# Output products with the weight as the stationary operand, and the result turned back on the way out

## The chip, the cores and the metric

The kernel runs on one core of one Trainium2 chip. The metric is device time in microseconds (us), the median of three runs. A core has a matrix engine (TensorE, here PE, with its weight loads shown apart as PEld), a vector engine (DVE), a scalar engine (ACT), GpSimd (POOL) and an engine that only issues transfers (SP). A matrix product loads a stationary operand of 128 columns, then streams a moving operand past it; the result goes to PSUM, from which DVE or ACT must copy it before a transfer can store it.

## The reference

Per batch (4) and head (8), a complex state of 48 x 48 is decayed, updated with k and v and read with q over 768 steps. The heads' outputs, side by side, are the rows x (3072 x 384) of a gated feed-forward layer:

```
S_re, S_im = decay(S_re, S_im, a_t) + k_t v_t^T      y_t = q_t S_re
g = x @ w_gate ; silu = g / (1 + exp(-g))
out = (silu * (x @ w_val)) @ w_out                    # w_out: 1536 x 384, float32 result
```

## The kernel before

The steps are cut into 24 slabs of 128 positions, two slabs to a group, so 12 groups of 256 positions. For each group, stage_ops computes decays and rotations on DVE and ACT, slab_ops makes scores, state products and outputs on PE (line 691 and its neighbours) and leaves x for 256 positions, split into a high part xh and a low part xl that the fast matrix format can hold. Weights are split in the same way.

ffn_ops(g) then runs 12 steps f for each group, one for each 128 of the 1536 hidden columns:

- f1 (line 942): 18 products, each with 128 columns of w_gate or w_val as the stationary operand and the 256 positions of xh or xl as the moving one (128x256), into the PSUM tile gv;
- silu on ACT (line 948), the gating product on DVE (line 953), then the split of the gated tile into hh (cast) and hl (difference);
- f2 (line 976): for each half of the group, three products with 128 positions of hh or hl as the stationary operand and the 384 columns of w_out as the moving one (128x384), so six to a step. They add up over the 12 steps in two PSUM tiles p_po, one for each half.

After step 11, oe copies each half out of PSUM (ACT line 354 or DVE line 356), and os stores its 128 rows with one transfer from SP (line 990). Group 0 works with unsplit operands (two products of line 976 to a step), and groups 1 to 11 with split ones.

A planner (plan, lines 120 to 206) simulates all engines with a table of costs and due times and writes one fixed order for each engine. Every engine then takes its instructions in that order and waits in place where an operand is missing. On PE the order is f1 of step f+1, then f2 of step f, so that silu, gating and split of a step run beside other products; scores, state products and cumulations stand in between. Step 0 of a group's f2 writes the PSUM tiles that oe of the group before must have read.

Some tiles are padded so that operands lie at chosen places: xh, xl, hh and hl have 128 columns more than they need and start 16 columns in (GATED, INPUT), and the f1 weights are allotted from a pool that a dummy tile of 96 columns (STILL) shifts. All other sizes are multiples of 128 columns. So the start of a moving operand lies, modulo 128 columns, 16 - 96 = 48 columns behind that of its stationary operand in f1, and 0 - 16 = 112 behind it in f2.

Of the kernel before, what the change touches and what calls it, by code (L numbers as in the profile page):

```python
# [9 lines left out]
F32 = mybir.dt.float32  # L10
# [44 lines left out]
WIDE_KEYS = 64  # L55
TURNS = P // WIDE_KEYS

TURN_OVER, STILL, GATED, INPUT = 128, 96, 16, 16
HIGH, LOW, WHOLE = 0, 1, 2
SHY = -5.6765  # L60
POOL_FROM = 9.8274
# [169 lines left out]
def quick(ctx, tc, q, k, v, a_re, a_im, w_gate, w_val, w_out, out, count):  # L231

    nc = tc.nc
    PS = bass.MemoryType.PSUM
    const = ctx.enter_context(tc.tile_pool(name="const", bufs=1))
    still = ctx.enter_context(tc.tile_pool(name="still", bufs=1))
    gap = ctx.enter_context(tc.tile_pool(name="gap", bufs=1))
    work = ctx.enter_context(tc.tile_pool(name="work", bufs=1))
    dram = ctx.enter_context(tc.tile_pool(name="dram", bufs=4, space=bass.MemoryType.DRAM))
    psum = ctx.enter_context(tc.tile_pool(name="psum", bufs=1, space=PS))  # L240
# [16 lines left out]
    G = const.tile([96, B, H, 64], F32, name="G")  # L257
    vts = [const.tile([P, H, 64], F32, name=f"vt{i}") for i in range(2)]
    turned_v = [const.tile([P, 2, 2, 64], F32, name=f"vr{i}") for i in range(2)]
    still.tile([P, STILL], F32, name="ahead")  # L260
    gap.tile([P, TURN_OVER - STILL], F32, name="behind")
    W, HALVES = {}, {}
    WIDE = {"w": 2 * DM, "o": DM}

    def place(nm, f, dtype):

        pool = still if nm == "w" else work
        return pool.tile([P, 2 * WIDE[nm]], dtype, name=f"w{nm}{f}", tag=f"w{nm}{f}", bufs=1)

    def spare(nm):  # L270

        if nm not in W:
            W.pop((nm, NF - 1, WHOLE))
            W[nm] = place(nm, NF - 1, F32)
        return W[nm]

    def weight(nm, f, part):
        at, n = "o" if nm == "o" else "w", DM if nm == "o" else 2 * DM
        if part == WHOLE:
            at = W[at, f, WHOLE].bitcast(F32).rearrange("p (n t) -> p n t", t=2)[:, :, 0]  # L280
# [38 lines left out]
    at_ = {}  # L319

    def new(tag, inst):
        if tag in fixed:
            t = fixed[tag][0]
        elif tag[0] in ("ww", "wo"):
            t = None
        elif tag in PSUMS:
            t = psum.tile([P, 512], F32, name="p_" + tag, tag=tag, bufs=2 if tag == "po" else slots[tag])
        else:
            shape, dt = SHAPE[tag]
            if isinstance(inst, tuple) and inst[0] in SPLIT:  # L330
                dt = F32R
            if tag == "xh" and inst == 0:
                dt = F32
            if tag == "xl" and isinstance(inst, str):
                dt = U32
            if tag in ("xh", "xl", "hh", "hl"):
                n = math.prod(shape[1:])
                ahead = GATED if tag in ("hh", "hl") else INPUT
                t = work.tile([P, n + TURN_OVER], dt, name=tag, tag=tag, bufs=slots[tag])[:, ahead:ahead + n]
                if len(shape) > 2:  # L340
                    t = t.rearrange("p (k n) -> p k n", k=shape[1])
            else:
                t = work.tile(shape, dt, name=tag, tag=tag, bufs=slots[tag])
                if tag == "dec":
                    t = t[:, 0:4 * H]
        at_[tag, inst] = t
        return t

    def tt(e, out, a, b, op=ALU.mult):
        V[e].tensor_tensor(out=out, in0=a, in1=b, op=op)  # L350

    def cast(e, out, in_):
        if e == "ACT":
            nc.scalar.copy(out=out, in_=in_)  # L354
        else:
            nc.vector.tensor_copy(out=out, in_=in_)  # L356
# [4 lines left out]
    def where(n):  # L361
        g, i = divmod(n, 2)
        c, bp = divmod(g, 2)
        return 2 * bp + i, c
# [237 lines left out]
    def slab_ops(n):  # L602
# [213 lines left out]
    def weight_ops(f):  # L816
        for nm, n, user in (("w", 2 * DM, "f1"), ("o", DM, "f2")):
# [34 lines left out]
            def whole(nm=nm):  # L852
                return W[nm, f, WHOLE].bitcast(F32).rearrange("p (n t) -> p n t", t=2)[:, :, 0]

            def c4(e, nm=nm, n=n, whole=whole):
                W.pop((nm, f - 1, WHOLE), None)
                W[nm, f] = place(nm, f - 1, F32R)
                cast(e, W[nm, f][:, 0:n], whole())

            def c5(e, nm=nm, n=n, whole=whole):  # L860
                tt(e, W[nm, f][:, n:2 * n], whole(), W[nm, f][:, 0:n].bitcast(F32), ALU.subtract)
# [64 lines left out]

    def ffn_ops(g):
        t0, step = (T1 + (g - 1) * NF * FT, FT) if g else (T0, FT0)
        for f in range(NF):
            I = f"{g}.{f}"  # L930
            key = t0 + f * step
# [33 lines left out]

            def f2(e, f=f, I=I):
                hh, hl, h = (at_.get((x, I)) for x in ("hh", "hl", "sg"))
                products = ((hh, HIGH), (hh, LOW), (hl, HIGH)) if g else ((h, WHOLE),)
                if f == 0:
                    new("po", f"{g}.0")  # L970
                    new("po", f"{g}.1")
                for i in range(2):
                    cs = slice(i * P, (i + 1) * P)
                    po = at_["po", f"{g}.{i}"][:, :DM]
                    for j, (l, part) in enumerate(products):
                        nc.tensor.matmul(out=po, lhsT=l[:, cs], rhs=weight("o", f, part),  # L976
                                         start=f == 0 and j == 0, stop=f == NF - 1 and j == len(products) - 1)
# [4 lines left out]
        for i in range(2):  # L982
            b, c = where(2 * g + i)
            I = f"{g}.{i}"

            def ev(e, I=I):
                cast(e, new("ost", I), at_["po", I][:, :DM])

            def st(e, I=I, b=b, c=c):
                nc.sync.dma_start(out=out[b * S + c * P:b * S + (c + 1) * P, :], in_=at_["ost", I])  # L990
# [69 lines left out]
    for g in range(1, NGRP):  # L1060
        ffn_ops(g)
# [175 lines left out]
```

## Time and profile before

| | |
|---|---|
| median of 3 runs | 629.52 us (629.48 to 631.21) |
| profiled execution | 629.75 us, span 628.0 us |
| PE busy | 600.1 us of the span, 96% |
| PEld, DVE, ACT busy | 566.9, 502.0, 405.2 us |
| chain that ended last | PE 83%, DVE 12% |
| f1 (line 942) and f2 (line 976) in that chain | 42% and 21% of the span |

The profiled execution is one run with the profiler on; 1.75 us of its time lie outside the span. A busy PE is pipelined: a product of 256 columns is shown as 0.28 us long, while the next one starts 0.11 us after it, so the pace is read from starts, not from durations.

### The profile page before, as it was taken

The page shows a single profiled execution, that of the slowest core. Times are in us where ns is not written, and L with a number is a line of the kernel's source. Part 1 is how long each engine was busy: PE and PEld are TensorE (multiplying, and loading weights), DVE is VectorE, ACT ScalarE, POOL GpSimd, SP SyncE. Part 2 cuts the span into 40 slices and gives each one's busy share as a digit, 9 for nine tenths or more (in the row PEclk, how much of TensorE's full clock was granted, in tenths as well). Part 3 has the DMA queues.
Part 4 walks back from the last instruction along what each step waited for, and adds up shares of the span by engine and source line. Part 5 has one row for each costly group of instructions (what it writes and reads, how often), then busy time and mean ns, then how long its engine had stood idle before and what let it go on. Part 6 is the DMA issues. An engine that isn't in the chain of part 4 may idle for free.

```text
span 628.0 us, 16113 instructions
## 1 busy us (share of the span) xinstructions
PE 600.1 (96%) x6562; PEld 566.9 (90%) x6562; DVE 502.0 (80%) x931; ACT 405.2 (65%) x653; POOL 4.2 (1%) x15
## 2 busy tenths in 40 slices
PE   2699999989999999999999999999999999999996
PEld 1488788978999899999999999999999999999995
DVE  8999999998997878977989869769879768544432
ACT  7865448886796794857876966976966873212210
POOL 2000000000000000000000000000000000000000
PEclk9999999999999999999999999999999999999999
DMA  8899501233635564455366453554464542331100
GB/s 258 230 301 310 204 27 32 64 124 85 161 106 147 132 149 123 129 139 139 91 148 148 108 153 95 144 156 95 136 166 113 146 121 70 101 103 51 52 1 30
DMA packets 155574, 79.89 MB, mean 127 GB/s; under 512 B 116187, under 2 KB 151261, under 8 KB 155494
## 3 DMA queue, kind: packets, MB, share of 16 engines
q1 hardware_dynamic: 155494, 78.80, 46.1%
q8 instruction: 53, 0.87, 0.6%
q14 instruction: 27, 0.22, 0.1%
HBM read 59.83 MB, written 4.78 MB: 103 GB/s over the span
## 4 chain that ended last, share of the span: by engine, by line
PE 83%; DVE 12%; DMA 1%; issue 1%; ACT 1%; SPq 1%; DVEq 0%
PE p_gv L942 42%; PE p_po L976 21%; PE p_py L691 6%; PE p_ps L691 6%; PE p_pm L503 2%; DVE ww L350 2%; PE p_pm L760 2%; PE p_gv L629 2%; DVE sg L953 1%; DVE s L350 1%; PE p_pm L757 1%; DMA wo<-in_q_dram 1%; DVE ks L350 1%; PE p_gv L500 1%; DVE wo L350 1%
## 5 line engine op out<-in xcount | busy, mean ns | idle before, releaser
L942 PE MATMUL p_gv<-xh,ww 128*128 128x256 f32 x1596 | 303.1, 287 | 2.0 <-DVE sg L953 1.3
L942 PEld LDWEIGHTS p_gv<-xh,ww 128*128 128x128 f32 x1596 | 256.0, 189 | 9.1 <-DVE sg L953 2.7
L942 PE MATMUL p_gv<-xl,ww 128*128 128x256 f32 x726 | 201.2, 277 | 0.0
L1068 ACT ACT_TABLE_LOAD x118 | 151.4, 1283 | 2.1
L942 PEld LDWEIGHTS p_gv<-xl,ww 128*128 128x128 f32 x726 | 136.3, 188 | 0.1
L948 ACT ACTIVATE sg<-p_gv 128x256 f32<-128x256 f32 x144 | 54.9, 384 | 123.7 <-PE p_gv L942 122.3
L976 PE MATMUL p_po<-wo,hh 128*128 128x384 f32 x484 | 125.1, 339 | 0.0
L953 DVE TENSOR_TENSOR sg<-sg,p_gv 128x256 f32<-128x256 f32 x144 | 59.0, 412 | 54.9 <-ACT sg L948 54.6
L976 PEld LDWEIGHTS p_po<-wo,hh 128*128 128x128 f32 x484 | 81.2, 188 | 1.6 <-issue 1.6
L976 PE MATMUL p_po<-wo,hl 128*128 128x384 f32 x242 | 80.7, 334 | 0.0
L350 DVE TENSOR_TENSOR hl<-sg,hh 128x256 fp32r<-128x256 f32 x132 | 54.9, 416 | 7.0 <-ACT hh L354 1.8
L976 PEld LDWEIGHTS p_po<-wo,hl 128*128 128x128 f32 x242 | 45.4, 188 | 0.0
L407 ACT ACTIVATE s<-s 128x768 f32<-128x768 f32 x44 | 36.7, 843 | 9.1 <-DVE s L350 6.7
L691 PEld LDWEIGHTS p_ps<-T 96*64 96x64 f32 x768 | 35.9, 138 | 5.0 <-issue 2.4
L691 PE MATMUL p_ps<-T 96*64 96x128 f32 (+1 forms) x768 | 39.4, 254 | 0.0
L719 DVE TENSOR_TENSOR sc<-p_ps,turn 128x512 f32<-128x512 f32 x48 | 32.1, 685 | 5.0 <-PE p_ps L691 4.8
L780 ACT CAST xh<-p_py 128x384 fp32r<-128x384 f32 x22 | 10.5, 480 | 37.6 <-PE p_py L691 37.5
L356 DVE CAST hh<-sg 128x256 fp32r<-128x256 f32 x87 | 25.2, 290 | 6.1 <-PE p_po L976 2.5
L354 ACT CAST hh<-sg 128x256 fp32r<-128x256 f32 x45 | 18.1, 404 | 18.3 <-DVE sg L953 14.4
L691 PE MATMUL p_py<-sc,vr 128*32 128x128 f32 x384 | 26.0, 273 | 0.9 <-issue 0.9
L691 PE MATMUL p_py<-sc,vt 128*32 128x128 f32 x384 | 25.2, 273 | 0.0
L942 PE MATMUL p_gv<-xh,ww-1_292 128*128 128x256 f32 x132 | 24.8, 280 | 0.0
(142 smaller groups left out, 853.9 us busy)
## 6 DMA issues: line engine op xcount, KB each, us to landing
T<-ww SPq DMA_DIRECT2D x216, 64.0 KB, 2.1
wo<-in_moe_w_out_dram SPq DMA_DIRECT2D x24, 384.0 KB, 4.4
ww<-in_moe_w_gate_dram SPq DMA_DIRECT2D x12, 384.0 KB, 5.8
ww<-in_moe_w_val_dram SPq DMA_DIRECT2D x12, 384.0 KB, 6.6
vt<-in_v_dram SPq DMA_DIRECT2D x24, 192.0 KB, 4.0
out_dram<-ost SPq DMA_DIRECT2D x24, 192.0 KB, 2.3
wo<-in_moe_w_gate_dram SPq DMA_DIRECT2D x12, 384.0 KB, 5.4
wo<-in_moe_w_val_dram SPq DMA_DIRECT2D x12, 384.0 KB, 3.6
```

The source lines that it names most:

```text
L350: V[e].tensor_tensor(out=out, in0=a, in1=b, op=op)
L354: nc.scalar.copy(out=out, in_=in_)
L356: nc.vector.tensor_copy(out=out, in_=in_)
L407: nc.scalar.activation(out=of(to or dst), in_=of(source), func=func, scale=scale, **kw)
L503: nc.tensor.matmul(out=ps, lhsT=tri, rhs=flat(half(x, i)), start=j == 0, stop=j == 1)
L691: nc.tensor.matmul(out=o, lhsT=l, rhs=r, start=opens, stop=closes, tile_position=(0, width * slot), skip_group_check=True)
L719: nc.vector.tensor_tensor(out=s.rearrange("p (r m) t -> p r m t", m=2), in0=scores[qd].rearrange("p (r m) t -> p r m t", m=2), in1=m, op=A ...
L942: nc.tensor.matmul(out=gv[:, i, :], lhsT=l, rhs=r, start=(m == 0), stop=(m == len(mm) - 1))
L948: nc.scalar.activation(out=new("sg", I), in_=at_["gv", I][:, 0:2 * P], func=AF.Silu)
L953: nc.vector.tensor_tensor(out=sg, in0=sg, in1=at_["gv", I][:, 2 * P:4 * P], op=ALU.mult)
L976: nc.tensor.matmul(out=po, lhsT=l[:, cs], rhs=weight("o", f, part), start=f == 0 and j == 0, stop=f == NF - 1 and j == len(products) - 1)
L1068: nc.scalar.preload_act_table_set(op.load)
```

## The change

In groups 1 to 10 the operands of f2 change places: 128 columns of w_out are stationary, and the 256 positions of hh or hl stream past them. A step then has nine products of 128x256 (three column blocks k, three parts each) where it had six of 128x384. The number of streamed columns stays 2304. Groups 0 and 11 ("upright") keep six products of 384 columns (group 0 two).

The result of the turned products has output columns on the partitions and positions along the row. oe turns it back with a DVE transpose of 32x32 blocks out of PSUM, whichever engine the planner had in mind. For the blocks to come out as rows of the result, the columns of w_out are stored in another order (rows_of, in c4 and c5, and undone for group 11's copies), and each half is stored by four transfers of 32 partitions by 4 by 96 elements, where one stored 128 rows of 384. The two PSUM tiles of a group become one tile of two banks. The dummy tiles go, and hh, hl, xh and xl start 48 columns in: f1 keeps its 48 columns, f2 of groups 1 to 10 has 48 as well, and f2 of group 11 has 0 - 48 = 80. The planner's costs and dependences are the same as before, so its order is too; only the instructions that a step issues differ.

```diff
-TURN_OVER, STILL, GATED, INPUT = 128, 96, 16, 16
+TURN_OVER, GATED, INPUT = 128, 48, 48
...
+    def rows_of(nm, at, plain=False):
+        if nm != "o":
+            return at
+        return at.rearrange("p (q k m) -> p q k m", k=KT, q=4) if plain else at.rearrange("p (k q m) -> p q k m", k=KT, q=4)
...
-            t = psum.tile([P, 512], F32, name="p_" + tag, tag=tag, bufs=2 if tag == "po" else slots[tag])
+            t = psum.tile([P, 1024 if tag == "po" else 512], F32, name="p_" + tag, tag=tag, bufs=slots[tag])
...
-                cast(e, W[nm, f][:, 0:n], whole())
+                cast(e, rows_of(nm, W[nm, f][:, 0:n]), rows_of(nm, whole(), True))
...
-                products = ((hh, HIGH), (hh, LOW), (hl, HIGH)) if g else ((h, WHOLE),)
...
-                for i in range(2):
-                    cs = slice(i * P, (i + 1) * P)
-                    po = at_["po", f"{g}.{i}"][:, :DM]
-                    for j, (l, part) in enumerate(products):
-                        nc.tensor.matmul(out=po, lhsT=l[:, cs], rhs=weight("o", f, part), ...
+                po = at_["po", g]
+                if upright:
...
+                    return
+                wh, wl = (weight("o", f, x).rearrange("p (k n) -> p k n", k=KT) for x in (HIGH, LOW))
+                for k in range(KT):
+                    for j, (l, r) in enumerate(((wh, hh), (wl, hh), (wh, hl))):
+                        nc.tensor.matmul(out=po[:, 2 * P * k:2 * P * k + 2 * P], lhsT=l[:, k, :], rhs=r,
+                                         start=f == 0 and j == 0 and k != 1, stop=f == NF - 1 and j == 2, skip_group_check=True)
...
-                cast(e, new("ost", I), at_["po", I][:, :DM])
+                if upright:
...
+                else:
+                    nc.vector.transpose(out=o.rearrange("p (j k m) -> p k j m", j=4, k=KT),
+                                        in_=po[:, 0:2 * P * KT].rearrange("p (k i j m) -> p k i j m", k=KT, i=2, j=4)[:, :, i])
...
+                for q in range(4):
+                    nc.sync.dma_start(out=r.rearrange("(j a) (q n) -> q a j n", a=32, q=4)[q],
+                                      in_=o[32 * q:32 * q + 32].rearrange("a (j n) -> a j n", j=4))
```

On PE, around step 0 of group 1's f2, before (ww are the f1 weights, xh and xl their moving operand, p_gv the sum of f1; wo is w_out, hh and hl the gated tile, p_po the sum of f2):

```order
L503 MATMUL p_pm<-s_956,tri 128x384
L503 MATMUL p_pm<-re,tri 128x384
L976 MATMUL p_po<-wo-1_344,hh 128x384 x2
L976 MATMUL p_po<-wo-1_344,hl 128x384
L976 MATMUL p_po<-wo-1_344,hh 128x384 x2
L976 MATMUL p_po<-wo-1_344,hl 128x384
L942 MATMUL p_gv<-xh,ww_880 128x256
L942 MATMUL p_gv<-xl,ww_880 128x256
```

and the same stretch now:

```order
L503 MATMUL p_pm<-s_947,tri 128x384
L503 MATMUL p_pm<-re,tri 128x384
L982 MATMUL p_po<-hh,wo-1_336 128x256 x2
L982 MATMUL p_po<-hl,wo-1_336 128x256
L982 MATMUL p_po<-hh,wo-1_336 128x256 x2
L982 MATMUL p_po<-hl,wo-1_336 128x256
L982 MATMUL p_po<-hh,wo-1_336 128x256 x2
L982 MATMUL p_po<-hl,wo-1_336 128x256
L943 MATMUL p_gv<-xh,ww_871 128x256
L943 MATMUL p_gv<-xl,ww_871 128x256
```

Six products of 384 columns became nine of 256, with the names on either side of the arrow exchanged, and nothing else moved around them. Groups 1 to 10 have 120 such steps.

On DVE, where group 1 ends and group 2's f2 is about to begin, before (flags are range checks, sg the gated tile, ks and qs the rotated k and q; line 953 is line 954 afterwards):

```order
L350 TENSOR_TENSOR ww_1390<-wo_1387,ww_1390 128x768
L446 TENSOR_REDUCE flags<-re 128x1
L923 TENSOR_REDUCE flags<-ww_1390 128x1
L953 TENSOR_TENSOR sg<-sg,p_gv 128x256
L350 TENSOR_TENSOR ks<-kt,s_1761 128x16x48
L350 TENSOR_TENSOR qs<-qt,s_1761 128x16x48
```

and now:

```order
L350 TENSOR_TENSOR ww_1404<-wo_1401,ww_1404 128x768
L446 TENSOR_REDUCE flags<-re 128x1
L923 TENSOR_REDUCE flags<-ww_1404 128x1
L998 STREAM_TRANSPOSE ost<-p_po 128x3x4x32 x2
L954 TENSOR_TENSOR sg<-sg,p_gv 128x256
L350 TENSOR_TENSOR ks<-kt,s_1784 128x16x48
L350 TENSOR_TENSOR qs<-qt,s_1784 128x16x48
```

Two transposes came in here, where ACT had two copies.

On SP, between two pieces of the same transfer of T (the turned q and k of a slab, 12 transfers; vr and vt are v, s the carry of phases), in group 3, before:

```order
L658 DMA T<-ww_1390 32x8x64 x3
L680 DMA vr_89<-in_v_dram 64x2x48 x4
L990 DMA out_dram<-ost 128x384
L658 DMA T<-ww_1390 32x8x64 x9
L990 DMA out_dram<-ost 128x384
L549 DMA s_3320<-fr 128x768
L666 DMA vt_87<-in_v_dram 128x8x48
```

and now:

```order
L658 DMA T<-ww_1404 32x8x64 x3
L680 DMA vr_83<-in_v_dram 64x2x48 x4
L1007 DMA out_dram<-ost 32x4x96 x4
L658 DMA T<-ww_1404 32x8x64 x9
L1007 DMA out_dram<-ost 32x4x96 x4
L549 DMA s_3439<-fr 128x768
L666 DMA vt_81<-in_v_dram 128x8x48
```

The nine later pieces of T stand behind four stores instead of one, and what comes after behind eight instead of two.

## Rows read from the trace of the kernel before

**Rows 1.** Page, part 1: busy us (share) and instructions of each engine.

```profile
PE 600.1 (96%) x6562; PEld 566.9 (90%) x6562; DVE 502.0 (80%) x931; ACT 405.2 (65%) x653; POOL 4.2 (1%) x15
```

**Rows 2.** Busy us (instructions) of each engine by stretch, clock, transfers.

```profile
97.00:160.00 63.00, 59.59 (x678) 54.97 (x678) 59.85 (x109) 48.97 (x76) 0.00 (x0) 1.00 0.32 86
...
280.00:400.00 120.00, 120.00 (x1474) 117.50 (x1472) 100.94 (x185) 90.56 (x140) 0.00 (x0) 1.00 0.49 126
```

**Rows 3.** All waits of PE, 165 to 620 us: total, times, longest.

```profile
PE p_gv L942 <- DVE sg L953: 1.3, 2, 0.9
```

**Rows 4.** Timeline of PE, 400 to 403 us: start, length, instruction.

```profile
400.00 0.39 PE L942 MATMUL p_gv<-xh,ww 128*128 128x256 f32 x2
400.22 0.28 PE L942 MATMUL p_gv<-xl,ww 128*128 128x256 f32 x1
400.34 0.39 PE L942 MATMUL p_gv<-xh,ww 128*128 128x256 f32 x2
...
401.47 0.51 PE L976 MATMUL p_po<-wo,hh 128*128 128x384 f32 x2
...
402.51 0.28 PE L942 MATMUL p_gv<-xh,ww 128*128 128x256 f32 x1
402.63 0.28 PE L942 MATMUL p_gv<-xl,ww 128*128 128x256 f32 x1
402.75 0.39 PE L942 MATMUL p_gv<-xh,ww 128*128 128x256 f32 x2
402.98 0.28 PE L942 MATMUL p_gv<-xl,ww 128*128 128x256 f32 x1
```

**Rows 5.** DVE by line and shape: busy us, mean ns, idle before.

```profile
L649 DVE STREAM_TRANSPOSE ww<-ks 128x768 f32<-128x768 f32 x18 | 17.5, 973 | 1.7 <-DMA T<-ww 1.6
...
L356 DVE COPY ost<-p_po 128x384 f32<-128x384 f32 x16 | 8.6, 548 | 1.7 <-PE p_po L976 1.7
...
L356 DVE CAST wo<-wo 128x384 fp32r<-128x384 f32 x7 | 2.5, 352 | 0.0
```

**Rows 6.** Timeline of DVE, 164 to 173 us.

```profile
164.01 0.94 DVE L923 TENSOR_REDUCE flags<-ww 128x1 f32<-128x768 f32 x1
164.87 0.41 DVE L953 TENSOR_TENSOR sg<-sg,p_gv 128x256 f32<-128x256 f32 x1
...
172.73 0.41 DVE L953 TENSOR_TENSOR sg<-sg,p_gv 128x256 f32<-128x256 f32 x1
```

**Rows 7.** Timeline of PE, the same stretch.

```profile
165.34 0.51 PE L976 MATMUL p_po<-wo-1_344,hh 128*128 128x384 f32 x2
...
173.19 0.39 PE L942 MATMUL p_gv<-xh,ww 128*128 128x256 f32 x1 [0.45 <-DVE sg L953]
```

**Rows 8.** Timeline of DVE, end of group 5.

```profile
403.43 0.55 DVE L356 COPY ost<-p_po 128x384 f32<-128x384 f32 x1
```

**Rows 9.** Timeline of PE, first product of group 6's f2.

```profile
404.57 0.51 PE L976 MATMUL p_po<-wo-1_344,hh 128*128 128x384 f32 x2
```

**Rows 10.** Timeline of all engines, the end of the program.

```profile
621.28 0.48 ACT L354 COPY ost<-p_po 128x384 f32<-128x384 f32 x1 [2.53 <-PE p_po L976]
621.43 0.34 PE L976 MATMUL p_po<-wo,hl 128*128 128x384 f32 x1
621.79 1.65 SPq L990 DMA_DIRECT2D out_dram<-ost  x2
621.81 0.56 DVE L356 COPY ost<-p_po 128x384 f32<-128x384 f32 x1 [1.75 <-PE p_po L976]
```

**Rows 11.** Timeline of SP, 263 to 271 us.

```profile
263.51 0.54 SPq L990 DMA_DIRECT2D out_dram<-ost  x1
264.10 5.87 SPq L658 DMA_DIRECT2D T<-ww  x9
```

**Rows 12.** Timeline of PE, first product that reads that T.

```profile
275.08 0.69 PE L691 MATMUL p_ps<-T 96*64 96x128 f32 x10
```

**Rows 13.** Page, part 6: issues, KB each, us to landing.

```profile
T<-ww SPq DMA_DIRECT2D x216, 64.0 KB, 2.1
```

More of the change, by code (lines that the diff above doesn't have):

```diff
@@ L235, in quick @@
     const = ctx.enter_context(tc.tile_pool(name="const", bufs=1))
-    still = ctx.enter_context(tc.tile_pool(name="still", bufs=1))
-    gap = ctx.enter_context(tc.tile_pool(name="gap", bufs=1))
     work = ctx.enter_context(tc.tile_pool(name="work", bufs=1))
@@ L259, in quick @@
     turned_v = [const.tile([P, 2, 2, 64], F32, name=f"vr{i}") for i in range(2)]
-    still.tile([P, STILL], F32, name="ahead")
-    gap.tile([P, TURN_OVER - STILL], F32, name="behind")
     W, HALVES = {}, {}
@@ L265, in place @@
     def place(nm, f, dtype):
-        pool = still if nm == "w" else work
-        return pool.tile([P, 2 * WIDE[nm]], dtype, name=f"w{nm}{f}", tag=f"w{nm}{f}", bufs=1)
+        return work.tile([P, 2 * WIDE[nm]], dtype, name=f"w{nm}{f}", tag=f"w{nm}{f}", bufs=1)
     def spare(nm):
@@ L857, in c4 @@
                 W[nm, f] = place(nm, f - 1, F32R)
-                cast(e, W[nm, f][:, 0:n], whole())
+                cast(e, rows_of(nm, W[nm, f][:, 0:n]), rows_of(nm, whole(), True))
             def c5(e, nm=nm, n=n, whole=whole):
-                tt(e, W[nm, f][:, n:2 * n], whole(), W[nm, f][:, 0:n].bitcast(F32), ALU.subtract)
+                tt(e, rows_of(nm, W[nm, f][:, n:2 * n]), rows_of(nm, whole(), True), rows_of(nm, W[nm, f][:, 0:n].bitcast(F32)), ALU.subtract)
             pl.add("c1" + N, cost(("DVE2",), n), c1, deps=loads + ([f"c3{f - 1}{nm}"] if f else []),
@@ L928, in ffn_ops @@
         t0, step = (T1 + (g - 1) * NF * FT, FT) if g else (T0, FT0)
+        upright = g in (0, NGRP - 1)
         for f in range(NF):
@@ L967, in f2 @@
                 hh, hl, h = (at_.get((x, I)) for x in ("hh", "hl", "sg"))
-                products = ((hh, HIGH), (hh, LOW), (hl, HIGH)) if g else ((h, WHOLE),)
                 if f == 0:
-                    new("po", f"{g}.0")
-                    new("po", f"{g}.1")
-                for i in range(2):
-                    cs = slice(i * P, (i + 1) * P)
-                    po = at_["po", f"{g}.{i}"][:, :DM]
-                    for j, (l, part) in enumerate(products):
-                        nc.tensor.matmul(out=po, lhsT=l[:, cs], rhs=weight("o", f, part),
-                                         start=f == 0 and j == 0, stop=f == NF - 1 and j == len(products) - 1)
+                    new("po", g)
+                po = at_["po", g]
+                if upright:
+                    products = ((hh, HIGH), (hh, LOW), (hl, HIGH)) if g else ((h, WHOLE),)
+                    for i in range(2):
+                        for j, (l, part) in enumerate(products):
+                            nc.tensor.matmul(out=po[:, 512 * i:512 * i + DM], lhsT=l[:, P * i:P * i + P], rhs=weight("o", f, part),
+                                             start=f == 0 and j == 0, stop=f == NF - 1 and j == len(products) - 1)
+                    return
[4 more added lines that the diff above has]
+                                         start=f == 0 and j == 0 and k != 1, stop=f == NF - 1 and j == 2, skip_group_check=True)
             PO = [("po", g)]
@@ L984, in ffn_ops, with ev @@
             I = f"{g}.{i}"
-            def ev(e, I=I):
-                cast(e, new("ost", I), at_["po", I][:, :DM])
-            def st(e, I=I, b=b, c=c):
-                nc.sync.dma_start(out=out[b * S + c * P:b * S + (c + 1) * P, :], in_=at_["ost", I])
+            def ev(e, i=i, I=I):
+                po, o = at_["po", g], new("ost", I)
+                if upright:
+                    part = po[:, 512 * i:512 * i + DM]
+                    cast(e, *((rows_of("o", x, plain) for x, plain in ((o, True), (part, False))) if g else (o, part)))
+                else:
+                    nc.vector.transpose(out=o.rearrange("p (j k m) -> p k j m", j=4, k=KT),
+                                        in_=po[:, 0:2 * P * KT].rearrange("p (k i j m) -> p k i j m", k=KT, i=2, j=4)[:, :, i])
+            def st(e, I=I, b=b, c=c):
+                r, o = out[b * S + c * P:b * S + (c + 1) * P, :], at_["ost", I]
+                if upright:
+                    nc.sync.dma_start(out=r, in_=o)
+                    return
+                for q in range(4):
+                    nc.sync.dma_start(out=r.rearrange("(j a) (q n) -> q a j n", a=32, q=4)[q],
+                                      in_=o[32 * q:32 * q + 32].rearrange("a (j n) -> a j n", j=4))
             key = t0 + NF * step + 4
```

## The prediction

> **What bounds the kernel now.** I read the shares of busy time first, then the stretches, then who waits for whom, then single instructions. PE is busy for 600.1 of 628.0 us [rows 1], but that is an average over two regimes. From 97 to 160 us DVE works without a break, 59.85 of 63 us, and PE is the one that waits; from 280 to 400 us PE has no idle time at all, with a granted clock of 1.00, which is the 2.4 GHz level [rows 2]. Over 165 to 620 us all of PE's own waits add up to 1.3 us, both of them for DVE's gating product [rows 3]. So from about 173 us on a nanosecond taken from PE's stream is a nanosecond of the total, and before that only DVE's chain counts.
>
> **What f2 costs, and what it would cost turned.** I take starts, because a product's length overlaps the next one's. In f1 three products of 256 columns run from 400.00 to 400.34, 113.3 ns each [rows 4]. The six products of f2 take 401.47 to 402.51, 1.04 us, 173 ns each [rows 4]. In streamed columns that is 0.443 ns against 0.451 ns. The turned step streams the same 2304 columns in nine products of f1's own form: 128 weight columns stationary, 256 positions moving, operands 48 columns apart as in f1. At f1's pace it takes 9 x 113.3 = 1.02 us, 0.020 us less.
>
> There is a second, smaller piece. The first four f1 products after an f2 take 402.51 to 402.98, 0.47 us, where four at f1's pace take 0.453 [rows 4]: about 0.015 us is lost where the width changes from 384 to 256. With one width everywhere that goes too.
>
> Steps that count: groups 2 to 10 have 108, three of them before 173 us, leaving 105; by the order of PE 76 of these are followed directly by an f1. So 105 x 0.020 + 76 x 0.015 = 2.1 + 1.1 = 3.2 us less. Bounds for the turned product, which no row shows: at best the bare stream, 256 columns at 2.4 GHz = 107 ns, so a step of 0.96 us and 8.4 + 1.1 = 9.5 us less; at worst the 120 ns of f1's first product after an f2 (402.51 to 402.63), a step of 1.08 us and 4.2 us more. I take 113.3, since operands, widths and distance are those of that row. Group 1's twelve steps lie in DVE's regime and count nothing (at most 0.4 us less).
>
> The Trainium skill (TensorE: Matmul & The Clock Gate, Back-to-back issue gap) speaks against the change: warm products follow each other after the columns over 2.4 GHz plus a fixed 2.5 ns, so nine narrow ones lose 7.5 ns to six wide ones; by that estimate the 105 steps would take 0.8 us more instead of 2.1 us less. The trace differs from it: 113.3 and 173 ns, 6.6 and 13 ns above the bare stream, so the surplus is not fixed here.
>
> The three extra weight loads of a step lie under the streams, as f1's do at 113.3 ns with one load per product.
>
> **What the copies cost.** A DVE copy of a half out of PSUM takes 548 ns; the one transpose that the trace has, 768 elements inside SBUF, takes 973 ns [rows 5], about what elementwise work of that size takes. So I put a 384-element transpose at 0.55 us, two in a row at 0.95 because DVE's instructions overlap a little. Bounds: 0.5 and 0.97 us each. Before, 14 of these 20 copies were on DVE and six on ACT; now all 20 are on DVE. Mostly this is hidden: at the end of group 5 the second copy starts at 403.43 and ends at 403.98, and the first product that overwrites that PSUM tile comes at 404.57 [rows 8, 9], 0.6 us later. A transpose may now only start when all nine products are done, which holds back the first of the two, but the second, on which the product waits, started after the last product before as well. The cover breaks if one transpose takes more than about 0.85 us.
>
> At one place there is no cover. Group 1 ends in DVE's regime: its two copies ran on ACT, and DVE went without a gap from the range check at 164.01 to the gating product at 164.87 and, over eleven more instructions that each start before the one ahead has ended, to the gating product at 172.73, whose end at 173.14 frees the buffer for which PE waited until 173.19 [rows 6, 7]. Two transposes now stand between the first two of these. Queued behind them are that gating product, the rotations and so PE's f1. They push 173.19 back by their whole 0.95 us; PE's first stall is at 165.34, f2's step 0 of group 2, which would start near 166.0, and it lies inside that delay. Cost: 0.95 us (0 if DVE's chain has slack that I don't see, 1.9 if a transpose takes 0.97).
>
> **The end.** Before, ACT copied the first half at 621.28 while PE still made the second, and DVE copied the second at 621.81, after the last product of 621.43 [rows 10]. With one PSUM tile for both halves, ACT's copy waits for the last product and DVE's for ACT's: the 0.48 us of ACT's copy moves onto the path. Cost 0.5 us (0.4 to 0.8, the copies now having a broken pattern).
>
> **Costs I put at nothing.** SP issues 60 more transfers. A store of a half takes SP 0.54 us and a T piece 5.87 / 9 = 0.65 [rows 11], so four small stores delay what is behind them by some 2.0 us. In group 3 nine pieces of T stand there; the last is issued near 269.4, lands 2.1 us later [rows 13], near 271.5, and is read at 275.08 [rows 12]. The cover of 3.6 us shrinks to 1.6; if it went altogether, the excess would be a PE stall at two or three boundaries. The reordered w_out halves keep their number of elements; their DVE casts run at 352 ns for 384, the fast form [rows 5]. If that form were lost, the seven would take the 548 ns of an ordinary pass, 1.4 us in DVE's regime, and no row excludes it; a gain is excluded, since the old pattern was the simplest one. I take 0, because the number of elements and engines is the same.
>
> f1's distance stays at 48 columns but both its operands move. I take no change; 1 ns either way on some 1,900 f1 products would be 1.9 us. Group 11's f2 goes from a distance of 112 to 80: 72 products, at 3 ns either way 0.2 us.
>
> **Sum.** -3.2 + 0.95 + 0.5 = -1.75 us. The profiled execution took 629.75 us, 0.23 above the median of 629.52, so against the median I forecast 627.8 us. A measurement of this kernel can tell about 0.3% from no change, 1.9 us, so the forecast lies just at that edge.
>
> **Rivals.**
> - The gain without its price: DVE's chain near 165 us absorbs the transposes. PE's only 0.45 us of idle time at 173.19 speaks for a chain that is barely longer than PE's; DVE's unbroken row speaks against. -3.2 + 0.5 gives 626.8 us.
> - No gain in the pace: f2's surplus comes from what it sums into or from the w_out tiles and not from the width, so that nine products also take 1.04 us, 116 ns each. Only the change of width is saved: -1.1 + 0.95 + 0.5 = +0.35, 629.9 us. For it: f1 is the only row of that form. Against: that row has 113.3 without fail.
> - Slower: each product carries a surplus that w_out as the stationary operand makes as large as after a change of width, 120 ns. Then 105 steps cost 4.2 us more: 4.2 + 0.95 + 0.5 = +5.65 with the loss after f2 kept, 635.2 us. With the loss of width gone, 0.35 us are to be earned back, so it decides from a pace of (1.04 - 0.35 / 105) / 9, some 115 ns, on. Against it: nothing in f1's operands differs in kind.
>
> **Chances.** Forecast 0.42 (half of it beyond the 0.3% mark), gain without price 0.28 (nearly all beyond it), no gain in the pace 0.18, slower 0.09, something else 0.03. That makes 0.44 for faster by over 0.3%, 0.42 for within 0.3%, 0.14 for slower. Around the forecast f1's place and the transposes give about 1.9 us either way, and the range reaches to the second and third case: 625.2 to 630.8 us.
>
> **What would show it.** In the profile after, from about 280 us on: f2 steps of nine products at 1.02 us, and an f1 with no slow first products, so that a pair takes 3.06 instead of 3.10 us. Near 165 us: two transposes of about 0.55 us on DVE, f2's step 0 near 166.0, the wait that ended at 173.19 about 0.95 longer or later. At the end: ACT's copy after the last product, DVE's after ACT's. On SP: four stores of about 0.6 us, and no wait of PE for T. The prediction is wrong if the pace of the nine differs from f1's by more than 2 ns, if f1's own pace moves with the new places, if a transpose takes near 1 us, or if PE waits at the other group ends.

## The result, and the profile after

The changed kernel is slower: 636.49 us against 630.17 us in the same comparison, a ratio of 1.0101 with an interval of 1.0082 to 1.0119. That is 6.3 us more, where 1.75 us less was forecast; it lies outside the range. The profiled execution took 636.82 us, with a span of 635.1 us.

The page, part 1, answers to [rows 1]:

```profile
PE 600.0 (94%) x6922; PEld 566.1 (89%) x6922; DVE 503.8 (79%) x937; ACT 403.1 (63%) x647; POOL 4.2 (1%) x15
```

PE has 360 instructions more and the same busy time, while the span grew by 7.1 us. So in sum the loss is idle time of PE, and the stretch where it had none shows it (busy us, instructions, then clock, transfers, as in [rows 2]):

```profile
280.00:400.00 120.00, 117.08 (x1527) 114.22 (x1527) 96.29 (x178) 85.89 (x136) 0.00 (x0) 0.99 0.54 125
```

All waits of PE from 165 to 620 us, against the single row of [rows 3] (p_py and sc belong to the state products):

```profile
PE p_gv L943 <- DVE sg L954: 5.5, 4, 2.6
PE p_po L982 <- DVE ost L998: 0.6, 1, 0.6
PE p_po L982 <- DVE hl L350: 0.6, 1, 0.6
PE p_py L691 <- DVE sc L719: 0.3, 1, 0.3
```

What the forecast said of single instructions is there. PE at 405 to 407 us, against [rows 4] (start, length, instruction):

```profile
405.98 0.28 PE L943 MATMUL p_gv<-xh,ww 128*128 128x256 f32 x1
406.09 0.39 PE L982 MATMUL p_po<-hh,wo 128*128 128x256 f32 x2
406.32 0.28 PE L982 MATMUL p_po<-hl,wo 128*128 128x256 f32 x1
...
407.11 0.28 PE L943 MATMUL p_gv<-xh,ww 128*128 128x256 f32 x1
```

Nine turned products take 406.09 to 407.11, 1.02 us. The transposes as a group by line, against [rows 5], and their first pair in DVE's timeline, against [rows 6]:

```profile
L998 DVE STREAM_TRANSPOSE ost<-p_po 128x384 f32<-128x384 f32 x20 | 10.8, 564 | 1.1 <-PE p_po L982 1.1
```

```profile
164.39 1.03 DVE L998 STREAM_TRANSPOSE ost<-p_po 128x384 f32<-128x384 f32 x2
165.35 0.38 DVE L954 TENSOR_TENSOR sg<-sg,p_gv 128x256 f32<-128x256 f32 x1
```

564 ns each, and two in a row push the gating product back by 0.96 us. At the end, against [rows 10]:

```profile
628.31 0.34 PE L976 MATMUL p_po<-wo,hl 128*128 128x384 f32 x1
628.68 0.48 ACT L354 COPY ost<-p_po 128x384 f32<-128x384 f32 x1 [3.06 <-PE p_po L976]
...
629.19 0.56 DVE L356 COPY ost<-p_po 128x384 f32<-128x384 f32 x1 [2.26 <-ACT ost L354]
```

ACT's copy now follows the last product and DVE's follows ACT's. What the forecast did not have is on SP and DVE near 320 us. SP there, against the pattern of [rows 11]:

```profile
310.69 1.96 SPq L1007 DMA_DIRECT2D out_dram<-ost  x4
312.69 5.88 SPq L658 DMA_DIRECT2D T<-ww  x9
318.67 3.19 SPq L1007 DMA_DIRECT2D out_dram<-ost  x4
321.97 0.36 SPq L549 DMA_DIRECT2D s<-fr  x1
322.38 0.43 SPq L890 DMA_DIRECT2D wo<-in_moe_w_gate_dram  x1
```

The same in the kernel before, where one store stands in each place:

```profile
311.50 5.87 SPq L658 DMA_DIRECT2D T<-ww  x9
317.47 0.54 SPq L990 DMA_DIRECT2D out_dram<-ost  x1
```

DVE in the changed kernel in the same stretch, and the product of PE that waited for it:

```profile
318.58 0.56 DVE L356 CAST s<-im 128x768 fp32r<-128x768 f32 x1
321.96 0.98 DVE L649 STREAM_TRANSPOSE ww<-ks 128x768 f32<-128x768 f32 x1 [2.82 <-DMA out_dram<-ost]
322.86 0.38 DVE L954 TENSOR_TENSOR sg<-sg,p_gv 128x256 f32<-128x256 f32 x1
...
323.30 0.38 PE L943 MATMUL p_gv<-xh,ww 128*128 128x256 f32 x1 [2.59 <-DVE sg L954]
```

The transpose of the next slab's ks writes the one spare buffer ww from which the T pieces of this slab are sent, so by the program it waits for T to have left. The row names a store, which uses the semaphore of an earlier T piece again; what landed just before DVE went on, at 321.57, is the last T piece. Behind the transpose in DVE's order stands the gating product, and for that one PE waits 2.59 us. In the kernel before the last T piece was issued 1.2 us earlier, landed at 318.79, and the same transpose follows without a wait:

```profile
318.98 0.97 DVE L649 STREAM_TRANSPOSE ww<-ks 128x768 f32<-128x768 f32 x1
```

So the cover that mattered was 0.2 us. The other late stalls (371.28, 424.10, 462.47) are of this kind too: DVE stands at a range check whose load from SP is late, or at a ks transpose.

A piece issued 1.2 us later does not by itself explain a wait of 2.8 us. With the last T piece landed 2.1 us after its issue, as fifteen of its sixteen parts were, DVE would have gone on near 320.5 us, by an estimate from the rows below. The trace counts the landing of each transfer in sixteen parts (us):

| transfer | issued | fifteen parts landed | last part | packet of 16 KB of instructions | DVE goes on |
|---|---|---|---|---|---|
| last T piece, changed | 317.97 | 320.07 | 321.57 | 319.02 to 320.53 | 321.96 |
| load for a range check, changed | 416.59 | 420.32 | 422.67 | 419.07 to 420.72 | 422.70 |
| last T piece, changed | 457.74 | 459.84 | 460.75 | 458.13 to 459.49 | 461.13 |
| load for a range check, changed | 364.23 | 369.34 | 369.39 | | 369.42 |
| last T piece, before with four stores | 317.73 | 319.76 | 319.80 | none before 325.74 | 320.19 |

In three of the four late stalls of the changed kernel DVE waited 0.9 to 2.4 us for one part in sixteen, each time with a packet of instructions in transfer. Late parts are in every kernel (the last part came over 0.6 us after the fifteenth in 38 of 252 T pieces and range-check loads before, in 50 afterwards, in 34 with one store), so what is new is where they fall and that no cover hides them. The last row, from the second experiment below, has no late part, and its transpose waited 1.51 us all the same, so the issues alone are enough for such a wait. That the packet of instructions delays the part is argued from the times; no run tests it.

DVE's waits for transfers by line, in the changed kernel from 165 to 620 us:

```profile
DVE flags L894 <- DMA wo<-in_moe_w_gate_dram: 7.1, 5, 2.5
DVE flags L894 <- DMA wo<-in_moe_w_val_dram: 5.6, 2, 3.3
DVE ww L649 <- DMA out_dram<-ost: 4.5, 2, 2.8
DVE ww L649 <- DMA T<-ww: 1.8, 2, 0.9
```

Before, the largest were 2.1 us for the range-check loads and 1.6 us for T.

Where the time lies can be added up on PE, since each product's time to the start of the next belongs to one part (waits over 0.15 us apart, as the profile has them). The numbers are us, rounded, from one profiled execution of each kernel; "one store" is the first experiment below:

| | before | changed | one store | four stores, 1536 bytes |
|---|---|---|---|---|
| start of group 2's f1 | 156.7 | 156.3 | 156.0 | 156.9 |
| f1, groups 2 to 10 | 224.4 | 224.8 | 224.8 | 227.6 |
| f2, groups 2 to 10 | 114.9 | 113.9 | 113.5 | 113.9 |
| f1 and f2, group 11 | 37.2 | 38.0 | 38.0 | 38.0 |
| all other products | 86.8 | 88.3 | 86.5 | 87.4 |
| PE's stalls | 1.3 | 7.0 | 2.4 | 5.8 |
| from the last product's start on | 6.5 | 6.8 | 6.9 | 6.9 |
| span | 628.0 | 635.1 | 628.0 | 636.5 |

Two things stand out: PE's stalls, of which the four late ones above make 4.4 us, and f1, which in group 11 costs more and elsewhere gains nothing, though f2 became cheaper. The experiments take them in this order. The changed kernel's f1 and f2 also hold some 1.7 us that the lower granted clock cost after the stall near 323 us, by the rows in the last section.

### The profile page after: what moved, and what is told of

It is laid out like the page before. It is cut to its first block, busy times and chain, and to the rows that moved or that the text cites. A ratio compares the mean times of both kernels' runs of the same rounds, so it can differ in the third digit from the quotient of the medians.

```text
span 635.1 us, 16898 instructions
## 1 busy us (share of the span) xinstructions
PE 600.0 (94%) x6922; PEld 566.1 (89%) x6922; DVE 503.8 (79%) x937; ACT 403.1 (63%) x647; POOL 4.2 (1%) x15
## 4 chain that ended last, share of the span: by engine, by line
PE 66%; DVE 13%; DMA 8%; ACT 5%; SPq 5%; issue 2%; DVEq 0%; ACTq 0%
PE p_gv L943 34%; PE p_po L982 14%; PE p_py L691 5%; PE p_ps L691 4%; PE p_po L976 3%; PE p_pm L503 2%; ACT L1086 2%; DVE ww L350 2%; PE p_pm L760 2%; DMA wo<-in_moe_w_gate_dram 2%; SPq L658 2%; DMA ww<-in_moe_w_val_dram 1%; ACT s L407 1%; DVE sg L954 1%; DMA re<-in_a_re_dram 1%
## 5 line engine op out<-in xcount | busy, mean ns | idle before, releaser
L949 ACT ACTIVATE sg<-p_gv 128x256 f32<-128x256 f32 x144 | 54.9, 384 | 114.9 <-PE p_gv L943 112.8
L982 PE MATMUL p_po<-hh,wo 128*128 128x256 f32 x660 | 119.7, 279 | 0.0
L982 PEld LDWEIGHTS p_po<-hh,wo 128*128 128x128 f32 x660 | 101.1, 189 | 1.6 <-issue 1.6
L982 PE MATMUL p_po<-hl,wo 128*128 128x256 f32 x330 | 91.7, 278 | 0.6 <-DVE hl L350 0.6
L982 PEld LDWEIGHTS p_po<-hl,wo 128*128 128x128 f32 x330 | 62.3, 189 | 0.8 <-DVE hl L350 0.8
L894 DVE TENSOR_REDUCE flags<-wo 128x1 f32<-128x384 f32 x36 | 19.5, 543 | 13.8 <-DMA wo<-in_moe_w_gate_dram 7.1
L899 ACT ACTIVATE wo<-wo 128x384 f32<-128x384 f32 x36 | 20.0, 557 | 11.8 <-DMA wo<-in_moe_w_gate_dram 6.3
```

Source lines behind the costliest of these rows:

```text
L894: nc.vector.tensor_reduce(out=flags[:, fl_lo + j:fl_lo + j + 1], in_=high(1), axis=AX.X, op=ALU.min, apply_absolute_value=True)
L899: nc.scalar.activation(out=high(0), in_=high(1), func=AF.Square, accum_out=flags[:, fl_hi + j:fl_hi + j + 1])
L949: nc.scalar.activation(out=new("sg", I), in_=at_["gv", I][:, 0:2 * P], func=AF.Silu)
L982: nc.tensor.matmul(out=po[:, 2 * P * k:2 * P * k + 2 * P], lhsT=l[:, k, :], rhs=r, start=f == 0 and j == 0 and k != 1, stop=f == NF - 1 an ...
```

## The experiments

**One store instead of four, in the changed kernel.**

```diff
-for q in range(4):
-    nc.sync.dma_start(out=r.rearrange(...)[q], in_=o[32 * q:32 * q + 32]...)
+nc.sync.dma_start(out=r, in_=o)
```

> The changed kernel with one store for each half of groups 1 to 10, as before, instead of four; the pieces of a row then land in the wrong places of the output (that part of the computation is changed), everything else, the transposes too, stays. Theory A (the four stores hold up what SP has queued behind them, T pieces and range-check loads, and DVE waits for these in order): 628.4 us, at most 629.4, the forecast's -1.75 against 630.2; no wait of 2.8 us of DVE's transpose ww<-ks near 319 us, DVE's waits for the range-check loads back from 13.8 to some 2 us, granted clock without a drop near 325 us. Rival B (the transposes themselves: more work on DVE at each group's end): 634 to 637 us, as the changed kernel. Rival D (more instructions on PE, so more instruction fetches that collide with transfers): 633 to 637 us.

630.17 us, ratio 1.0014 (1.0003 to 1.0025). 5.5 us of the loss are gone (1.0101 - 1.0014 of 629.5 us), the transposes and the additional products are not, so rivals B and D fall (both kernels move 56 packets of instructions by their pages, so it isn't their number). The expected 628.4 was not reached: 0.9 us slower than before is left. All of PE's waits from 165 to 620 us:

```profile
PE p_gv L943 <- DVE sg L954: 1.8, 3, 0.9
PE p_po L982 <- DVE ost L998: 0.6, 1, 0.6
```

**Four stores in the kernel before.**

```diff
-nc.sync.dma_start(out=out[b * S + c * P:b * S + (c + 1) * P, :], in_=at_["ost", I])
...
+for q in range(4):      # groups 1 to 10
+    nc.sync.dma_start(out=r.rearrange(...)[q], in_=o[32 * q:32 * q + 32]...)
```

> The kernel before, with nothing changed but the stores of groups 1 to 10: four of 32 partitions by 4 by 96 elements, as in the changed kernel, instead of one (the pieces land in the wrong places of the output). Theory A: the price of the stores is what the changed kernel lost and what its products won, 6.3 + 1.75 = 8 us if the waits are the same, so 636 to 639 us, at least 633; DVE waits for T before a transpose ww<-ks and for the range-check loads. Rivals B and D: 630 us, as before.

632.18 us, ratio 1.0052 (1.0033 to 1.0072): slower by 3.3 us, in the direction of theory A, under half of its size and below the 633 us that it set as the least. The same instructions wait, for shorter times:

```profile
DVE flags L894 <- DMA wo<-in_moe_w_val_dram: 4.7, 3, 2.6
DVE flags L894 <- DMA wo<-in_moe_w_gate_dram: 3.7, 3, 2.4
DVE ww L649 <- DMA out_dram<-ost: 3.5, 2, 2.0
```

So the price of 60 issues is no constant. By the times above it depends on where they, and the late parts, fall among the other engines' work; no run separates the two.

**Issue time or packets.** One store of the changed kernel's packet size, and four of before's:

```diff
+r = r.rearrange("p (j n) -> (p j) n", j=4).rearrange("(j p) n -> p j n", j=4)
+nc.sync.dma_start(out=r, in_=o.rearrange("p (j n) -> p j n", j=4))
 # and, in the other kernel:
+for q in range(4):
+    nc.sync.dma_start(out=r[32 * q:32 * q + 32], in_=o[32 * q:32 * q + 32])
```

> The changed kernel with one store for each half of groups 1 to 10, but in packets of 384 bytes: 128 partitions by 4 by 96 elements (the pieces land in the wrong places of the output). SP issues as often as in the kernel with one store, the transfer engines get 512 packets a half as in the changed kernel. Theory A (it is SP's issue time): 630.2 us, at most 631.5, PE's stalls after 165 us 3 us or less. Rival A2 (it is the small packets): 633.5 us or more, T pieces issued as early as with one store but landed later.

> The changed kernel with four stores for each half of groups 1 to 10, each of 32 partitions with their whole rows of 1536 bytes (the pieces land in the wrong places of the output). SP issues as often as in the changed kernel, the packets are those of the kernel before. Theory A: 634 to 638 us, with PE's stalls near 323, 424 and 462 us. Rival A2: 630 to 631 us.

630.14 us, ratio 1.0012 (1.0001 to 1.0023), and 636.93 us, ratio 1.0101 (1.0079 to 1.0122). The page's queue rows of the two, in the same order (packets, MB, share), show what was exchanged:

```profile
q1 hardware_dynamic: 163174, 78.80, 48.4%
```

```profile
q1 hardware_dynamic: 156454, 78.80, 48.0%
```

Four times as many packets in one issue cost nothing; four issues of large packets cost what the changed kernel costs. Theory A2 falls: it is the issues on SP's queue that cost. That the second sum equals the changed kernel's is in part luck. Its stalls are 5.8 us where the changed kernel has 7.0, and its f1 takes 2.8 us more, by the pace that comes below.

**Another place in SP's queue.** Three kernels move the stores of groups 1 to 9 in SP's order and leave all else:

```diff
 order = pl.plan()
+for g in range(1, NGRP - 1):    # each store behind a later operation of SP
...
+        order.insert(to, order.pop(at))
...
-t = work.tile(shape, dt, ..., bufs=slots[tag])
+t = work.tile(shape, dt, ..., bufs=3 if tag == "ost" else slots[tag])    # not in the first
```

> The changed kernel with all of its instructions, only the four-fold stores of groups 1 to 9 stand later in SP's order: behind the store of the last row of phases (line 582), or behind the next loads, where SP has idle time, and not ahead of T pieces and range-check loads. Theory A: 628.4 us, at most 630; what counts is who stands behind the stores. Rival A2 (small packets of the stores, 128 by 384 bytes each in place of 1536, load the transfer engines wherever they stand): 633 us or more. Rivals B and D: 634 to 637 us.

> The kernel whose stores stand behind the store of the last row of phases (line 582), now with three buffers ost instead of two, so that DVE's transposes no longer wait 4.1 and 1.2 us for stores of the group before. If those waits were what made that order slow: its 638.5 us less the stall of 5.2 us at 216 us, 633 to 634 us, PE's stalls after 165 us 3 to 4 us. If the place itself is bad (T pieces and range-check loads come late there as well): 636 us or more.

> The changed kernel with three buffers ost instead of two, so that no transpose waits for a late store, and with the four-fold stores of groups 1 to 6 each placed behind the next load of q or k (line 397), where SP has idle time before and after; those of groups 7 to 9 behind the next loads. All other instructions and orders stay. Theory A (SP's issue time ahead of T pieces and range-check loads): 630 to 631 us, the time of the kernel with one store; PE's stalls after 165 us add up to 2.4 us or so instead of 7.0. Rival A2 (the small packets cost wherever they stand): 633 us or more, with T pieces that land late though issued in time.

All three missed: 638.52 us (1.0158, 1.0134 to 1.0182), 637.04 us (1.0104, 1.0077 to 1.0130) and 641.44 us (1.0181, 1.0166 to 1.0197). In the first the stall at 323 us is gone, but DVE's transposes wait 4.1 and 1.2 us for the late stores of the group before, and PE 5.2 us at 216 us. With a third buffer one transpose still waits 3.3 us for a store, and PE 3.0 us. In the last the place that I took for idle lies just ahead of all twelve T pieces, and DVE's waits for T are the largest so far (its timeline with SP's and DVE's rows, and the row of its waits):

```profile
305.42 3.15 SPq L1007 DMA_DIRECT2D out_dram<-ost  x4
308.67 1.97 SPq L658 DMA_DIRECT2D T<-ww  x3
...
322.15 0.98 DVE L649 STREAM_TRANSPOSE ww<-ks 128x768 f32<-128x768 f32 x1 [2.68 <-DMA T<-ww]
```

```profile
DVE ww L649 <- DMA T<-ww: 8.6, 5, 2.8
```

The place does decide, as theory A has it, but idle time in SP's row is no cover: here SP stood idle only until DVE had filled the buffer, at 306.18 us, and the stores put there held up T until 308.67.

**The stores from GpSimd.**

```diff
-    nc.sync.dma_start(out=r.rearrange(...)[q], ...)
+    nc.gpsimd.dma_start(out=r.rearrange(...)[q], ...)
```

> The changed kernel with the four-fold stores of groups 1 to 10 issued from GpSimd, which is busy for 4 of 635 us, instead of SP; the transfers themselves are the same. Theory A: 628.4 us, 627.5 to 630: SP's rows as before. Rival A2 (the packets, not SP's issue time): 633 us or more. Rival: GpSimd's issue is slow or takes DVE's port, price unknown, seen in DVE's durations near the group ends. Rivals B and D: 634 to 637 us.

633.24 us, ratio 1.0065 (1.0044 to 1.0087), between the two. An issue takes GpSimd 0.55 us (548 ns at the median of 80), and DVE's transposes near the group ends stay at 565 ns, so nothing shows that these issues hold DVE up. PE's stalls fall from 7.0 to 3.4 us, the largest 1.68 us at 457.5, again behind a ks transpose that waits for T; the last of T's sixteen parts landed at 455.82, 1.5 us after the fifteenth. Of the 3.1 us that separate it from one store, 1.0 us are stalls; products of f1 and f2 take 1.8 us more, by the pace that comes next.

**Group 1 upright, with one store.**

```diff
-upright = g in (0, NGRP - 1)
+upright = g in (0, 1, NGRP - 1)
...
```

> The kernel with one store for each half (wrong places in groups 2 to 10), with group 1 upright as well, so that no transposes stand where DVE has no cover. The forecast's term of 0.95 us: 629.2 us, silu of group 2's fifth step about 0.9 us earlier than with group 1 turned, measured from the first step of that group. Rival (DVE's chain has slack there): 630.2 us.

630.84 us, ratio 1.0028 (1.0009 to 1.0046): no gain in the total. The term itself is there. From the silu of group 2's first step to that of its fifth, the kernel before takes 13.45 us, one store with group 1 turned 14.38, and with group 1 upright 13.45, so the transposes cost 0.93 us at that place. In the profiled executions PE's stalls are 1.8 us shorter than with one store and group 1 turned, but group 2's f1 starts 1.2 us later, the other products take 0.8 us more, and f1 takes 0.7 us more: its steps of group 2, from 157 to 192 us, run at 117.7 ns a product instead of 113.3.

**The pace of 256 columns.** PE in the run with one store, in group 10:

```profile
569.06 0.40 PE L943 MATMUL p_gv<-xh,ww 128*128 128x256 f32 x2
569.30 0.28 PE L943 MATMUL p_gv<-xl,ww 128*128 128x256 f32 x1
569.41 0.40 PE L943 MATMUL p_gv<-xh,ww 128*128 128x256 f32 x2
569.65 0.28 PE L943 MATMUL p_gv<-xl,ww 128*128 128x256 f32 x1
569.77 0.40 PE L943 MATMUL p_gv<-xh,ww 128*128 128x256 f32 x2
570.00 0.28 PE L943 MATMUL p_gv<-xl,ww 128*128 128x256 f32 x1
570.12 0.28 PE L943 MATMUL p_gv<-xh,ww 128*128 128x256 f32 x1
```

Nine products take 569.06 to 570.12, 117.7 ns each, at a granted clock of 1.00. So the same product has two paces. In the run with one store, from 173 us on, it is the slow one from 207 to 212 us, from 353 to 361, from 504 to 548 and from 568 on, and 113.3 in the steps between. There it changes only at an interruption, the products of line 691 in between or, at 352.76, a single product that took 200 ns; once slow, it goes on through f1 and f2. The kernel before has slow steps of f1 as well (at 510.94 us a step takes 2.118 us), but single ones, and all of its group 11 is fast. Four kernels change only where operands start, modulo 128 columns:

```diff
 # before, hh and hl 32 columns later
-TURN_OVER, STILL, GATED, INPUT = 128, 96, 16, 16
+TURN_OVER, STILL, GATED, INPUT = 128, 96, 48, 16
 # before, f1's two operands both 32 columns later
+TURN_OVER, STILL, GATED, INPUT = 128, 128, 16, 48
 # one store, hh and hl 32 columns earlier
+TURN_OVER, GATED, INPUT = 128, 16, 48
 # one store, f1's operands where the kernel before has them
+TURN_OVER, STILL, GATED, INPUT = 128, 96, 48, 16
```

> The kernel before with one constant changed: hh and hl start 48 columns in instead of 16, so the wide products of f2 stand at 0 - 48 = 80 columns, as in group 11 of the changed kernel, instead of 112; f1 keeps its 48. Theory P (products of 256 columns have two paces, 113.3 and 117.7 ns, and the wide products at 112 columns bring them back to the fast one, those at 80 don't): f1 of group 11 takes 25.4 us instead of 24.7, and other stretches of f1 stay at 117.7 ns once they fell into it; 631 to 635 us. Rival P2 (the width alone brings the fast pace back; the slow pace of group 11 comes from elsewhere): 629.5 us, f1 of group 11 at 24.7 us.

> The kernel before with x and the f1 weights at the changed kernel's places: modulo 128 columns the moving operand of f1 stands at 16 and the stationary one at 96 (before 112 and 64), so f1 keeps its distance of 48 and f2 its 112, and only what changes between f1 and f2 differs. Theory X (the change of places between f2 and f1 brings the fast pace back, not the distance or the width within f2): f1 of group 11 at 25.4 us instead of 24.7, f1 of groups 2 to 10 above 225.5 us, 631 to 633 us. Rival W (wide products at a distance of 112 bring it back): f1 of group 11 at 24.7 us, 629.3 us.

> The kernel with one store for each half (the pieces of a row in the wrong places) with one more constant changed: hh and hl start 16 columns in instead of 48. The turned products then stand at 16 columns, group 11's wide ones at 112 as before. Theory P: f1 of group 11 at 24.7 us instead of 25.4; if a change of distance between f1 and f2 is enough to bring the fast pace back, the stretches at 117.7 ns from 504 to 545 and from 568 us go too, and the time falls from 630.2 to 628.0 to 629.0 us. If one width is what keeps the slow pace going, they stay: 629.4 us by group 11 alone. Rival P2: 630.2 us, nothing changes.

> The kernel with one store for each half (the pieces of a row in the wrong places), with f1's operands at the places that they had before: moving 112, stationary 64 modulo 128 columns; the turned products stay at 16 and 96. Every product still has a distance of 48, but each change between f1 and f2 is a change of places. Theory X: the slow pace no longer survives a step; f1 of groups 2 to 10 at or below 223 us instead of 224.8 and of group 11 at 24.7, no stretch at 117.7 ns from 502 to 545 us, 628 to 629 us. Rival W (with one width the slow pace goes on): 630.2 us, the stretches stay.

| | f1, groups 2 to 10 | f2 | f1, group 11 | ratio to before |
|---|---|---|---|---|
| before | 224.4 | 114.9 | 24.67 | 1 |
| hh and hl 32 later (distance 80) | 227.6 | 114.4 | 25.08 | 1.0047 (1.0032 to 1.0063) |
| both operands of f1 32 later | 229.2 | 114.7 | 25.49 | 1.0091 (1.0067 to 1.0116) |
| one store | 224.8 | 113.5 | 25.41 | 1.0014 (1.0003 to 1.0025) |
| one store, hh and hl 32 earlier (distance 16) | 226.8 | 116.4 | 25.39 | 1.0088 (1.0068 to 1.0108) |
| one store, f1 at before's places | 227.1 | 116.2 | 25.15 | 1.0065 (1.0045 to 1.0085) |

Each is slower than the kernel that it comes from, by 3 to 6 us. Theory P falls: group 11's wide products at a distance of 112 columns did not bring the fast pace back, and in the kernel before with 80 columns about half of the steps of f1 are slow, in group 11 every second one. Rival W falls too: f1 and f2 keep their distances in the second kernel, and f1 loses 4.8 us. Theory X holds there (25.49 us in group 11, though the time, 635.02 us, was above what was expected) and fails in the last kernel, where a change of places at every step left f1 slow and made f2 slow as well. So where the operands of f1 and f2 start counts, and not the distance within a product alone. By what rule is left open, and each pace was read from one profiled execution.

**Together.**

```diff
 # the kernel with stores at SP's idle places, and
+upright = g in (0, 1, NGRP - 1)
...
+ahead = (16 if inst.startswith("11.") else GATED) if tag in ("hh", "hl") else INPUT
```

> The kernel of the run with stores at SP's idle places, with group 1 upright as well (copies and one store for each half, no transposes where DVE has no cover) and with hh and hl of group 11 starting 16 columns in, so that its wide products have the distance of 112 columns that they had before. If each price is what the runs so far show: 0.95 us less for group 1, 0.8 us less in group 11, where the products of f1 took 117.7 ns instead of 113.3, so 628.3 to 629.3 us, level with the kernel before or a little faster. Rival A2: 631 us or more.

642.52 us, ratio 1.0197 (1.0180 to 1.0214). The place of the stores was the wrong one, as above, and f1 of group 11 stayed at 25.40 us. No version that the runs point to beats the kernel before.

## Why the prediction was wrong

- **The failing step is "0 for SP's 60 extra issues", under "Costs I put at nothing".** It measured 5.5 us. The extra issue time was right in kind: four stores took 1.96 us at 310.69, 1.4 more than one, where a delay of some 2.0 was forecast, and SP's issues sum to 324.9 us before and 360.8 after. Wrong was what their cover was measured against. The forecast took the first product of PE that reads T [rows 12], 3.6 us after landing; and indeed PE never waits for T. But the first to wait for those transfers is DVE, which reuses the spare buffer that they read, and there the cover near 320 us was 0.2 us. The sign stood in [rows 5]: of DVE's 1.7 us of idle time before that transpose, 1.6 ended with T. The loads of the range checks, behind the same queue, have readers on DVE and ACT that take their work in order. Either stops the gating product behind it. "No wait of PE for T" was the wrong thing to look for. And the landing was taken as 2.1 us after the issue [rows 13], a median: the T piece of the longest stall had a part that landed 3.6 us after it.
- **The pace of f2 was right, the pace of f1 was not.** f2 takes 1.02 us a step, as forecast. From 173 to 511 us the run with one store gains 2.35 us in 84 steps, 0.028 us each where 3.2 / 105 = 0.030 was forecast. Then it loses 1.6 us again up to 610 us. Of the 3.2 us, f2 brought 1.5 and f1 nothing (0.3 us more instead of 1.1 less), and group 11's f1 took 0.74 us more, a place that had been costed by f2 alone at 0.2. "That row has 113.3 without fail" was a reading of too few rows: the trace of before has the slow pace in single steps. The Trainium skill (TensorE: Matmul & The Clock Gate, Back-to-back issue gap) gives a fixed gap of 2.5 ns for products by themselves, and says that in a stream of weight loads and products both set the spacing, which the forecast left out. The rows have 6.6 and 11 ns above the bare stream for one and the same shape, so neither its estimate nor the forecast's, each with one number, could give the time.
- **The transposes: right.** 564 ns, and 0.93 us in DVE's regime for the 0.95 forecast. At the other group ends they hid, as argued: the one wait of PE that names them, 0.6 us, is the one near 165 us.
- **The end: right in kind**, 0.3 to 0.4 us for the 0.5 forecast.
- **The casts: right**, 353 ns for the seven.
- **The rivals.** None named SP. The forecast's one sentence on it, in the costs, gave the excess to "two or three boundaries" as PE stalls; the stalls came, four of them, but through DVE.

## What to carry to other kernels

A transfer has two ends: what waits for its data, and what waits for its source to be free again. When issues are added to a queue, list every operation behind them, and take the smallest cover over both kinds of waiters, including in-order engines whose wait holds unrelated work. A cover of a few tenths of a microsecond is none where single parts of a transfer land 1 to 2 us after the rest. And a pace read from one stretch is a sample: look over all steps of that form for a second value before multiplying it by a hundred.

## What the runs showed of the hardware

- A wait of PE can cost more than itself. After the 2.59 us that ended at 323.30 the granted clock fell to the lower level, 1.2 GHz; the rows by 2 us (PE busy first, the clock third from the end):

```profile
322.00:324.00 2.00, 0.70 (x6) 0.70 (x7) 2.00 (x3) 0.70 (x2) 0.00 (x0) 1.00 0.71 137
324.00:326.00 2.00, 2.00 (x14) 2.00 (x13) 1.40 (x5) 1.95 (x4) 0.00 (x0) 0.59 0.90 206
326.00:328.00 2.00, 2.00 (x12) 2.00 (x11) 0.04 (x1) 0.04 (x1) 0.00 (x0) 0.56 1.18 248
328.00:330.00 2.00, 2.00 (x54) 1.79 (x54) 1.36 (x3) 1.97 (x4) 0.00 (x0) 1.00 0.83 143
```

  From the silu near 319.6 us to the second one after it (at 332.11 us before, 336.53 in the changed kernel) the changed kernel falls back by 4.3 us, of which 2.6 are the stall. The same drop followed stalls of 1.96 us (four stores of 1536 bytes), 3.0 and 5.2 us (stores later), and none followed 2.44 and 2.79 us (stores at idle places), so the length of one stall alone does not say.
- One part in sixteen can land late. In three traces in which the ks transpose near 320 us waited over 2 us (the changed kernel, four stores of 1536 bytes, stores at idle places), a packet of 16 KB of instructions (1.51 us in the changed kernel, at 319.02) fell among the last T packets, and the last part of the last T piece landed 1.5, 1.0 and 1.3 us after its fifteenth. In the kernel before the packet came after T, at 323.46, and T landed whole.
- One shape of product, 128x256, ran at 113.3 and at 117.7 ns at the same granted clock, in stretches of over 40 us, and shifting operands by 32 columns moved the sum over f1 of nine groups by up to 4.8 us.
